# Hash attention and a squared-ReLU layer by two-level Winograd products: an earlier request for the next x, later inner weight factors, and another order in the last output product

## The chip, the cores and the metric

The kernel runs on one core of one Trainium2 chip. The metric is device time in microseconds (us) for one execution, as the median of several runs. The core has TensorE (PE, with its weight loads shown as PEld), VectorE (DVE), ScalarE (ACT), GpSimd (POOL) and SyncE (SP). SP, ACT and POOL issue DMA transfers, each on a queue of its own (in the profile q1, q10 and q0).

## The reference

Attention whose scores are kept only where the hash buckets of query and key agree, then a layer `x @ w_in`, squared ReLU, `@ w_out`:

```python
mask = q_bucket[:, :, :, None] == k_bucket[:, :, None, :]
scores = np.where(mask, scale * np.matmul(q, k.transpose(0, 1, 3, 2)), -1000000000.0)
attn = np.exp(scores - np.max(scores, axis=-1, keepdims=True))
attn = attn / (np.sum(attn, axis=-1, keepdims=True) + 1e-09)
x = (attn @ v).transpose(0, 2, 1, 3).reshape(B * S, H * D)   # 3072 x 512
h = x @ w_in                                                 # 512 x 2048
out = (np.maximum(h, 0.0) ** 2) @ w_out                      # 2048 x 512
```

All tensors are float32. There are 4 batches, 8 heads, 768 positions and 64 features a head; six hash bits come from the signs of `q @ proj` and `k @ proj`.

## The kernel before

The kernel is written out by hand in program order: on every engine the instructions run in the order in which the Python code emits them, and waits on semaphores are put in where a tile is reused or read. Nothing reorders them later.

**Stages.** The first 330 us are attention, two heads at a time. Its result goes to DRAM as `x_all`. Meanwhile the weights are brought into factors for Winograd's form of a block product (seven products and some sums in place of eight products). Then the second layer runs over three chunks of 1024 rows of x (`NCHUNK` is 3, index `i`). A chunk has two parts: the hidden part (`hidden` in the first chunk, `hidden_pair` in the others) makes the squared-ReLU blocks `b11`, `b12`, `b21`, `b22`, `b_t`, and `project(i)` makes the output from them.

**Output products.** `project` runs seven outer products, `k` from 0 to 6 (product 0 to product 6 below). Each is again a Winograd product, made by `product` (L703): seven adds, each of them four matmul calls that use one *leaf* (a 128x512 tile, 256 KB, a factor of `w_out`). An fp32 call shows as two matmuls in the profile, so an add is eight matmuls. The adds take leaves in the order 0, 1, 4, 3, 5, 6, 2 and use three PSUM accumulators; between them ACT copies accumulators out (`one`, `two`, `five`, `three`), and DVE adds them up through `c11`, `c12`, `c22` and `c21`, which stand for the four blocks of the product's result. Leaf n of the chunk (n counts from 0 over all products) is loaded five adds ahead by `load_leaf`, on SP for the first five of a first chunk and on ACT's queue after that; there are seven leaf buffers.

**The hook.** After the second add `product` calls `hook` (L1133). Its first subtraction, `minus(y21, y21, t2)` at L516, makes the right-hand side "t4", which the product's seventh add reads. Then `inner_sums(k + 1)` makes the sums for the next product (three subtractions).

**x and the inner factors.** There is one buffer for x, `load_x(i)` (L551) fills it with 2 MB through POOL's queue, and `sum_x` after products 3 and 4 makes sums of it for the next chunk. From the second chunk on, half of the hidden part is a Winograd product of two levels. Its inner weight factors are made once, in the first chunk's `project`, by `factor_units(n)` (L836) for n from 0 to 3: two loads of 256 KB through POOL into buffers named `h`, four DVE sums (L510 to L513), and four stores to DRAM (L849), again through POOL. `load_inner` reads them back from product 6 on. The `h` buffers are five, taken in turn, and the output blocks use the same ones.

**The end.** In the last product of a chunk (`fourth`) c11 and c12 complete one half of a block of the output and c22 and c21 the other. `close` sends a half when it has both: by a DVE transpose (L1025) and eight small transfers, or, for the second half in the last chunk, by `put_last` (L1037), which transposes on PE, copies on ACT (column 1) and DVE (column 0) and issues two transfers each on SP and ACT.

**Queues.** POOL's queue carries, in this order around the first `project`: stores of the output factors (L1194), the loads of `raw_qk` (L752), then `factor_units` and `load_x`. SP carries `w_unit` (the weights of a hidden step, 640 KB each here), the first leaves and most of the output.

Of the kernel before, what the change touches and what calls it, by code (L numbers as in the profile page):

```python
# [34 lines left out]
def kernel(  # L35
# [31 lines left out]
    NCHUNK = B * S // NCH  # L67
# [14 lines left out]
    HF, HD, NR, NQ = DFF // 2, DM // 2, NFF // 2, NFF // 4  # L82
# [462 lines left out]
    for pr in range(NIN // 2, NP):  # L545
        n = 16 if pr == NP - 1 else 1 + (pr % 3 == 0)
# [4 lines left out]
    def load_x(i):  # L551

        x = p_c.tile([P, NFT, NCH], FP32, name="x")
        nc.gpsimd.dma_start(out=x, in_=x_all[:, :, i * NCH:(i + 1) * NCH])
        xs[i] = x, [p_c.tile([P, 2, NCH // 2], FP32, name=f"t_x{n}") for n in range(3)]
# [36 lines left out]
    with tc.manual_schedule():  # L592
# [21 lines left out]
        for pr in range(NP):  # L614
            a, b = 2 * pr, 2 * pr + 1
            more = pr + 1 < NP
# [83 lines left out]
            p_g.tile([P, NR, HN], FP32, name=f"b{n}") for n in ("11", "12", "21", "22", "_t")  # L700
        )

        def product(n, w, at, bt, c11, c12, c21, c22, hook=None, c22_first=False):  # L703

            acc = [ps_m.tile([P, 512], FP32, name=f"acc{i}")[:, 0:w] for i in range(3)]

            def add(to, a, b, first, last):  # L710
                for i in range(n):
                    nc.tensor.matmul(  # L712
                        out=acc[to], lhsT=a(i), rhs=b(i), start=first and i == 0,
                        stop=last and i == n - 1, skip_group_check=True,
                    )

            def keep(of, name):
                t = p_r.tile([P, 512], FP32, name=name)[:, 0:w]
                nc.scalar.copy(out=t, in_=acc[of])  # L719
                return t  # L720

            add(0, at(0), bt["11"], True, False)
            one = keep(0, "one")
            add(1, at(1), bt["21"], True, True)
            if hook:
                hook()
            c11(acc[1], one)
            add(0, at(4), bt["t2"], False, False)
            two = keep(0, "two")
            add(2, at(3), bt["t1"], True, False)  # L730
            five = keep(2, "five")
            add(0, at(5), bt["t3"], False, False)
            three = keep(0, "three")
            if c22_first:
                c22(three, five)
            add(2, at(6), bt["22"], False, True)
            c12(acc[2], two)
            if not c22_first:
                c22(three, five)
            add(0, at(2), bt["t4"], False, True)  # L740
            c21(acc[0])

# [60 lines left out]
        def new_h():  # L803
            return p_r.tile([P, HN], FP32, name="h", bufs=NH)
# [31 lines left out]
        def factor_units(n):  # L836

            src = [new_h().rearrange("p (a f c) -> p a f c", a=2, c=P) for _ in range(2)]
            for j in range(2):
                nc.gpsimd.dma_start(out=src[j], in_=w_in_7[j * NQ + n, :, 5:7])  # L840
            sums = [new_h().rearrange("p (a f c) -> p a f c", a=2, c=P) for _ in range(2)]
            sums_a(
                src[0][:, :, 0], src[0][:, :, 1], src[1][:, :, 0], src[1][:, :, 1],
                *(sums[j // 2][:, :, j % 2] for j in range(4)),
            )
            for lo, hi, t in (
                (0, 2, src[0]), (2, 3, src[1][:, :, 1:2]), (3, 5, sums[0]), (5, 7, sums[1])
            ):
                nc.gpsimd.dma_start(out=w_in_49[n, :, :, lo:hi], in_=t)  # L849
# [207 lines left out]
        def project(i):  # L1057

            V, W, U, X = (p_y.tile([P, 4, QN], FP32, name=f"sum{n}") for n in range(4))
            outs = {}  # L1060

            def out_block(ih, jh, n):

                row, col = n // 2, n % 2
                if (ih, jh, row) not in outs:
                    outs[ih, jh, row] = [p_y.tile([P, HN], FP32, name="o", bufs=NOUT), 0]
                o = outs[ih, jh, row]
                return o[0][:, col * QN:(col + 1) * QN]

            def close(ih, jh, n):  # L1070
                o = outs[ih, jh, n // 2]
                o[1] += 1
                if (i, ih, jh, n // 2) == (NCHUNK - 1, 1, 0, 1):

                    if o[1] == 2:
                        for col in (1, 0):
                            put_last(n - n % 2 + col, o[0][:, col * QN:(col + 1) * QN])
                elif o[1] == 2:
                    put_out(i, ih, jh, n // 2, o[0])

            def first_(n, one, two):
                if two is None:
                    nc.scalar.copy(out=block(V, n), in_=one)
                else:
                    add_to(block(V, n), one, two)

            def seventh(n, one, two):
                add_to(block(W, n), block(V, n), whole(one, two))

            def fifth(n, one, two):  # L1090
                if two is None:
                    nc.scalar.copy(out=block(U, n), in_=one)
                else:
                    add_to(block(U, n), one, two)

            def third(n, one, two):
                add_to(block(X, n), block(U, n), whole(one, two))
                add_to(block(X, n), block(X, n), block(V, n))

            def second(n, one, two):  # L1100
                add_to(out_block(0, 0, n), block(V, n), whole(one, two))
                close(0, 0, n)

            def sixth(n, one, two):
                t = whole(one, two)
                add_to(out_block(0, 1, n), block(X, n), t)
                close(0, 1, n)
                add_to(block(W, n), block(W, n), t)
                add_to(out_block(1, 1, n), block(W, n), block(U, n))
                close(1, 1, n)  # L1110

            def fourth(n, one, two):
                add_to(out_block(1, 0, n), block(W, n), whole(one, two))
                close(1, 0, n)

            more = i + 1 < NCHUNK
            uses = first_, seventh, fifth, third, second, sixth, fourth
            for k in range(7):
                b = OUTER[k][1]
                t1, t2 = tens.pop(k)  # L1120
                if i == 0 and k < NQ:
                    factor_units(k)
                if k == 6 and more:
                    load_inner(i + 1, 0)
                at = lambda m, k=k: lambda n: leaves[k, m][:, n]
                bt = {
                    "11": lambda n: b[:, n, 0:QN], "21": lambda n: b[:, NQ + n, 0:QN],
                    "22": lambda n: b[:, NQ + n, QN:HN], "t1": lambda n: t1[:, n],
                    "t2": lambda n: t2[:, n], "t3": lambda n: b[:, n, QN:HN],
                    "t4": lambda n: b[:, NQ + n, 0:QN],  # L1130
                }

                def hook():  # L1133
                    y21 = b[:, NQ:NR, 0:QN]
                    minus(y21, y21, t2)
                    if k + 1 < 7 and k not in (1, 3):
                        inner_sums(k + 1)
                    if k == 6 and more:
                        sums_inner(i + 1)

                counted = []

                def a_with_load(m, k=k):
                    load_leaf(7 * k + len(counted) + NLEAF - 2)
                    counted.append(m)
                    return at(m)

                use = uses[k]
                product(
                    NQ, QN, a_with_load, bt, lambda *p: use(0, *p), lambda *p: use(1, *p),  # L1150
                    lambda p: use(2, p, None), lambda *p: use(3, *p), hook, k == 6,
                )
                if k == 0 and i + 1 < NCHUNK:
                    load_x(i + 1)
                if k in (3, 4) and i + 1 < NCHUNK:
                    sum_x(i + 1, 2 * k - 5)
                    sum_x(i + 1, 2 * k - 4)
                if k == 5 and i + 1 == NCHUNK:
                    guard()
                if k == 0:  # L1160

                    for h in range(2):
                        at_h = slice(h * NQ, (h + 1) * NQ)
                        minus(b11[:, at_h], b22[:, at_h], b_t[:, at_h])
                    inner_sums(2)
                if k == 2:

                    for h in range(2):
                        at_h = slice(h * NQ, (h + 1) * NQ)
                        minus(b_t[:, at_h], b21[:, at_h], b11[:, at_h])  # L1170
                    inner_sums(4)
# [315 lines left out]
```

## Time and profile before

| what | us |
|---|---|
| median of 4 runs | 879.29 (878.71 to 880.27) |
| the profiled execution, whole | 879.31 |
| its span, first to last instruction | 877.5 |
| attention, weights | 0 to about 330 |
| hidden part of the first chunk | about 330 to 427.3 |
| output products of the first, second, third chunk start at | 427.3, 606.0, 783.6 |
| last matmul of the output products starts at | 868.4 |

Times in the views below count from the span's start. A row of a timeline has start, duration, engine, line, operation, what it writes and reads, how many instructions are merged in the row, and in brackets how long the engine was idle before it and what ended that. In a chain of waits each row is a start, a duration and the work that the end of the program hung on. Matmul ends are modelled, so the last tenth of a microsecond of a matmul row is not to be read closely.

The issues and landings around the first `project`, from the trace:

| transfer | issued | landed after |
|---|---|---|
| w_unit (SP, 640 KB) | 427.5 | 6.6 |
| leaf 5 | 427.90 | 6.8 |
| leaf 6 | 429.40 | 6.0 |
| leaf 7 | 429.78 | 6.3 |
| leaf 8 | 432.85 | 3.9 |
| stores of unit 0 (POOL, 2 of 256 KB) | 432.87 | 4.5 and 4.8 |
| x for the second chunk (POOL, 2 MB) | 434.00 | 12.2 |
| loads of unit 1 (POOL, 2 of 256 KB) | 434.76 | 12.4 and 12.8 |
| leaf 10 | 436.30 | 7.6 |
| leaf 11 | 436.72 | 9.3 |
| leaf 12 | 439.68 | 8.2 |
| x for the third chunk (POOL) | 614.97 | 12.8 |

### The profile page before, as it was taken

The numbers are of one execution on the slowest core, as the hardware profiler recorded it, in microseconds if no ns is written. First come the engines' busy times: TensorE is split into PE (matmuls) and PEld (weight loads), VectorE is DVE, ScalarE is ACT, GpSimd is POOL, SyncE is SP. The second block draws the span as 40 slices with busy tenths as digits, with TensorE's granted clock in tenths as the row PEclk, the third lists the DMA queues.
The fourth block names the chain that finished last, engine by engine and source line by source line (L and its number), as shares of the span: only waits on it lengthen the run. The fifth ranks groups of instructions, "written<-read, shape, count | busy, mean of one in ns | idle before, by whom it ended". The sixth has DMA issues, their size and how long they took to land.

```text
span 877.5 us, 12127 instructions
## 1 busy us (share of the span) xinstructions
PE 864.7 (99%) x4340; PEld 519.2 (59%) x4340; DVE 760.6 (87%) x1099; ACT 391.7 (45%) x673; POOL 106.9 (12%) x172
## 2 busy tenths in 40 slices
PE   8999999999999999999999999999999999999996
PEld 4444444444444444444688865556888755568885
DVE  5999999999999998888779968888889788888875
ACT  6888888888888852222211123332111233321110
POOL 2000000000000001554231011111000211110002
PEclk9999999999999999999999999999999999999998
DMA  9777977998878526999897764536846744355565
GB/s 174 150 146 133 222 168 150 190 253 226 178 175 227 163 97 220 294 267 284 293 349 240 182 161 167 173 118 222 285 149 188 167 164 155 126 167 151 161 172 108
DMA packets 224131, 167.09 MB, mean 190 GB/s; under 512 B 164448, under 2 KB 181344, under 8 KB 224064
## 3 DMA queue, kind: packets, MB, share of 16 engines
q1 hardware_dynamic: 189152, 87.19, 41.0%
q0 software_dynamic: 12528, 41.30, 15.2%
q10 hardware_dynamic: 22384, 37.76, 13.8%
q8 instruction: 36, 0.59, 0.3%
q14 instruction: 31, 0.25, 0.1%
HBM read 124.52 MB, written 41.68 MB: 189 GB/s over the span
## 4 chain that ended last, share of the span: by engine, by line
PE 95%; DVE 2%; ACT 1%; DMA 1%; issue 0%; POOL 0%; ACTq 0%; POOLq 0%; DVEq 0%
PE acc L712 40%; PE st L396 17%; PE acc L934 16%; PE xo L438 14%; PE acc L887 6%; PE hash L346 2%; PE tot L455 1%; DVE total L428 1%; DMA k_nat<-in_k_dram 1%; ACT bits L356 1%; ACT e L413 0%; PE xo L477 0%; PE tp L309 0%; DVE x_t L493 0%; DVE recs L487 0%
## 5 line engine op out<-in xcount | busy, mean ns | idle before, releaser
L413 ACT ACTIVATE e<-st 128x1024 f32<-128x1024 f32 x192 | 145.0, 810 | 44.9 <-PE st L396 41.0
L396 PE MATMUL st<-feat,feat 64*128 64x512 f32 (+1 forms) x768 | 150.4, 483 | 0.0
L438 PE MATMUL xo<-e,v_nat 128*64 128x512 f32 (+1 forms) x768 | 134.8, 492 | 0.0
L712 PE MATMUL acc<-b,leaf 128*128 128x256 f32 x600 | 133.3, 379 | 1.0 <-issue 1.0
L712 PEld LDWEIGHTS acc<-b,leaf 128*128 128x128 f32 x600 | 113.8, 190 | 17.5 <-issue 2.2
L428 DVE TENSOR_TENSOR total<-total,e 128x1536 f32<-128x1536 f32 x64 | 112.4, 1756 | 8.2 <-ACT e L413 3.6
L438 PEld LDWEIGHTS xo<-e,v_nat 128*64 128x64 f32 x768 | 51.3, 136 | 82.2 <-issue 74.3
L934 PE MATMUL acc<-t_x,w_unit 128*128 128x512 f32 x192 | 90.2, 592 | 0.0
L396 PEld LDWEIGHTS st<-feat,feat 64*128 64x128 f32 x768 | 66.0, 188 | 32.8 <-issue 23.2
L712 PE MATMUL acc<-t,leaf 128*128 128x256 f32 x336 | 76.2, 380 | 0.0
L356 ACT ACTIVATE bits<-hash,lifts 32x384 bf16<-32x384 f32 x120 | 68.7, 573 | 2.3 <-PE hash L346 0.4
L712 PEld LDWEIGHTS acc<-t,leaf 128*128 128x128 f32 x336 | 63.7, 190 | 9.1 <-DVE t L516 0.5
L799 DVE SCALAR_TENSOR_TENSOR b<-h 128x512 f32<-128x512 f32 x96 | 65.7, 692 | 3.0
L396 PE MATMUL st<-bits,bits 64*128 64x256 bf16 (+1 forms) x384 | 63.1, 325 | 1.7 <-ACT e L413 1.2
L934 PE MATMUL acc<-x,w_unit 128*128 128x512 f32 x128 | 60.1, 592 | 0.0
L712 PE MATMUL acc<-x,w_unit 128*128 128x512 f32 x128 | 56.6, 594 | 0.0
L712 PE MATMUL acc<-b_t,leaf 128*128 128x256 f32 x240 | 53.8, 379 | 0.0
L934 PEld LDWEIGHTS acc<-t_x,w_unit 128*128 128x128 f32 x192 | 36.5, 190 | 28.9 <-issue 26.8
L719 ACT COPY two<-acc 128x256 f32<-128x256 f32 (+1 forms) x29 | 12.5, 432 | 87.7 <-PE acc L712 72.2
L719 ACT COPY one<-acc 128x256 f32<-128x256 f32 (+1 forms) x29 | 12.5, 431 | 85.4 <-PE acc L712 56.7
L712 PEld LDWEIGHTS acc<-b_t,leaf 128*128 128x128 f32 x240 | 45.5, 190 | 6.2
L396 PEld LDWEIGHTS <-bits 64*128 64x128 bf16 x384 | 23.6, 93 | 42.5 <-issue 38.4
(159 smaller groups left out, 1166.9 us busy)
## 6 DMA issues: line engine op xcount, KB each, us to landing
leaf<-w_out ACTq DMA_DIRECT2D x142, 256.0 KB, 3.1
w_unit<-w_in SPq DMA_DIRECT2D x16, 640.0 KB, 4.0
raw<-in_moe_w_in_dram SPq DMA_DIRECT2D x16, 512.0 KB, 5.4
raw<-in_moe_w_out_dram SPq DMA_DIRECT2D x16, 512.0 KB, 4.5
w_unit<-w_in SPq DMA_DIRECT2D x8, 896.0 KB, 8.3
w_out<-sums POOLq DMA_DIRECT2D x16, 448.0 KB, 6.8
sum<-w_in SPq DMA_DIRECT2D x16, 448.0 KB, 5.1
v_nat<-in_v_dram SPq DMA_DIRECT2D x16, 384.0 KB, 4.3
```

What stands on the lines that cost most here:

```text
L346: nc.tensor.matmul(out=banks[g * NR_B:(g + 1) * NR_B, h, 0:HS], lhsT=projs[rows], rhs=feat[pr, w][rows, c * HS:(c + 1) * HS], start=True, ...
L356: nc.scalar.activation(out=t[h * D:h * D + NR_B, c * HS:(c + 1) * HS], in_=hashed[pr, w][at, h, 0:HS], func=ACTF.Sign, scale=HUGE, bias=li ...
L396: nc.tensor.matmul(out=st[:, h, 0:hi - lo], lhsT=src[pr, 1][rows, key], rhs=src[pr, 0][rows, lo:hi], start=first, stop=not first,)
L413: nc.scalar.activation(out=e[:, :, lo:hi], in_=sts[i][:, :, 0:hi - lo], func=ACTF.Exp, scale=scale)
L428: nc.vector.tensor_tensor(out=totals[pr], in0=totals[pr], in1=weights[pr, kt][:, :, 0:S], op=ALU.add)
L438: nc.tensor.matmul(out=xo[h * D:(h + 1) * D, lo:hi], lhsT=nat[pr, "v_nat"][:, h, kt * D:(kt + 1) * D], rhs=weights[pr, kt][:, h, lo:hi], s ...
L455: nc.tensor.matmul(out=tot[g * 32:(g + 1) * 32, 0:HS], lhsT=ones, rhs=totals[pr][:, h, c * HS:(c + 1) * HS], start=True, stop=True,)
L712: nc.tensor.matmul(out=acc[to], lhsT=a(i), rhs=b(i), start=first and i == 0, stop=last and i == n - 1, skip_group_check=True,)
L719: nc.scalar.copy(out=t, in_=acc[of])
L799: nc.vector.scalar_tensor_tensor(out=out, in0=h, scalar=0.0, in1=h, op0=ALU.max, op1=ALU.mult)
L887: nc.tensor.matmul(out=out, lhsT=w[:, a], rhs=b, start=start, stop=stop, skip_group_check=True)
L934: nc.tensor.matmul(out=acc[to], lhsT=w[:, PLACE[a], f], rhs=bt[b](f), start=first and f == 0, stop=last and f == NFT // 2 - 1, skip_group_ ...
```

## The change

Three edits. The keyword `c22_first` of `product` goes, so that in product 6 of each chunk `c22` is called after `c12`, as in the other products. `load_x(i + 1)` is called at the beginning of product 0, ahead of everything else of the product, where it was called after product 0. And `factor_units(0)` to `factor_units(3)` are called at the beginning of products 1 to 4, where they were called at the beginning of products 0 to 3.

```diff
-        def product(n, w, at, bt, c11, c12, c21, c22, hook=None, c22_first=False):
+        def product(n, w, at, bt, c11, c12, c21, c22, hook=None):
...
             three = keep(0, "three")
-            if c22_first:
-                c22(three, five)
             add(2, at(6), bt["22"], False, True)
             c12(acc[2], two)
-            if not c22_first:
-                c22(three, five)
+            c22(three, five)
             add(0, at(2), bt["t4"], False, True)
             c21(acc[0])
...
-                if i == 0 and k < NQ:
-                    factor_units(k)
+                if k == 0 and more:
+                    load_x(i + 1)
+                if i == 0 and 0 < k <= NQ:
+                    factor_units(k - 1)
                 if k == 6 and more:
                     load_inner(i + 1, 0)
...
-                    lambda p: use(2, p, None), lambda *p: use(3, *p), hook, k == 6,
+                    lambda p: use(2, p, None), lambda *p: use(3, *p), hook,
                 )
-                if k == 0 and i + 1 < NCHUNK:
-                    load_x(i + 1)
```

In the instruction streams this moves one transfer on POOL (x of the second chunk, from behind the six transfers of unit 0 to ahead of them), four sums on DVE in the first chunk (each unit's four stand one product later, so that four leave the front of product 0 and four are added in front of product 4's hook), and three pairs of rows on DVE, one for each chunk (c22's two adds, behind c12's two adds and its transpose). PE, ACT and SP keep their streams.

## The prediction

> **What bounds the kernel now.** I read the page first, then the waits of PE, then the chain of waits around the output products of the first chunk, then the timelines of DVE and POOL there, then the landings of the leaves, last the tail.
>
> ```profile
> span 877.5 us, 12127 instructions
> ...
> PE 864.7 (99%) x4340; PEld 519.2 (59%) x4340; DVE 760.6 (87%) x1099; ACT 391.7 (45%) x673; POOL 106.9 (12%) x172
> ```
>
> PE works 864.7 of 877.5 us. Matmuls are not touched, so a gain can only come from the 12.8 us in which PE stands, most of it before its first matmul and after its last. Inside, the chain has one break:
>
> ```profile
> 429.87 20.13 PE acc L712 x93
> 450.01 0.95 issue
> 450.96 62.40 PE acc L712 x288
> ```
>
> One add of an output product is 8 matmuls, 62.40/288*8 = 1.73 us; a product is seven adds, 12.1 us. The first matmul of product 0 is at 427.33 (PE's timeline), so product 1 begins at 439.4 and its seventh add is due at 427.33+13*1.73 = 449.8: just where the break is. That add reads the right-hand side "t4", which the hook's first subtraction (L516 b<-b,t) writes. DVE shows why it is late:
>
> ```profile
> 445.44 1.22 DVE L516 TENSOR_TENSOR b_t<-b_t 128x1024 f32<-128x1024 f32 x1
> 448.17 0.43 DVE L510 TENSOR_TENSOR h<-h 128x256 f32<-128x256 f32 x1 [1.51 <-DMA h<-w_in]
> ...
> 449.64 1.22 DVE L516 TENSOR_TENSOR b<-b,t 128x1024 f32<-128x1024 f32 x1
> ```
>
> The subtraction ends at 450.86, and PE starts 0.1 us later. In front of it stand the four sums of factor_units(1) (L510 to L513), and they waited 1.51 us for their load. POOL's timeline tells why that was late: it was issued just behind the 2 MB of the next x.
>
> ```profile
> 434.00 0.95 POOL L554 DMA_DIRECT2D x<-x_all  x1
> 434.76 1.28 POOL L840 DMA_DIRECT2D h<-w_in  x2
> 447.42 0.68 POOL L849 DMA_DIRECT2D w_in<-h  x1 [11.38 <-DMA h<-w_in]
> ```
>
> **Part 1, the stall: -0.95 us.** After the change POOL asks for x before any factor load, and the four sums ahead of product 1's hook are those of unit 0. x can go out when PE has read the old x for the last time, at 427.5 (426.48+1.02, the last matmul of hidden(0,7)); POOL's other wait, an older transfer on its queue, is long over. The two loads of unit 0 follow at 428.5 to 429.6. With the 12.4 and 12.8 us which the same pair took behind x before, they land by 442.4. DVE comes to the sums at 446.66 (445.44+1.22): it gets there no earlier than before, although four sums (1.47 us, from 448.17 to 449.64) leave its queue ahead of product 0, because c12 of product 0 started at 437.96, when PE had finished the sixth add (427.33+6*1.73 = 437.7). So: sums 446.66 to 448.1, hook to 449.35, wanted at 449.8. The stall goes, with 0.45 us to spare. The same chain (c12, c22, two b_t or b subtractions of 4.4, three of inner_sums 3.5, sums 1.47, hook 1.22: 11.4 us against 12.1) stands from product 2 to 3, where the hook ended at 474.69 against 475.1 wanted; it keeps that thin cover. Product 2's sums still wait for their load (3.15 us before); its hook ended at 459.4, wanted at 463.1, and that 3.7 us hides it. Product 4 gets the last four sums: its hook ended at 482.77, wanted at 487.4; 4.6 less 1.47 leaves 3 us. If one of these covers fails, what it is short by is PE's. The inner weights are next read by load_inner before product 6 (about 501), and unit 0 is stored by 454: late by nothing.
>
> For the second chunk nothing moves: ahead of x on POOL stand the loads of raw_qk in both kernels, and x is asked for at 614.97 either way. Bounds of part 1: 0 (hook still late) and -0.95; I take -0.95.
>
> **Part 2, the tail: +0.65 us.** No instruction is added, c22 goes behind c12 in the last product of each chunk. In the first two chunks DVE has the same sum of work before c21, and PE goes on with other work; nothing. At the very end:
>
> ```profile
> 865.82 0.42 DVE L1011 TENSOR_TENSOR tmp<-three,five 128x256 f32<-128x256 f32 x1 [1.22 <-ACT three L719]
> 866.28 0.43 DVE L1011 TENSOR_TENSOR o<-sum,tmp 128x256 f32<-128x256 f32 x1
> 867.09 0.42 DVE L1011 TENSOR_TENSOR tmp<-acc,two 128x256 f32<-128x256 f32 x1 [0.38 <-PE acc L712]
> ...
> 868.00 0.71 DVE L1025 STREAM_TRANSPOSE h<-o 128x512 f32<-128x512 f32 x1
> 868.81 0.42 DVE L1011 TENSOR_TENSOR o<-sum,acc 128x256 f32<-128x256 f32 x1
> ```
>
> The first two rows (c22) ran while DVE waited for PE. Afterwards c12 keeps 867.09 and its transpose 868.00; c22 starts at 868.64 and 869.05 (a row after a transpose starts 0.64 after it, a dependent one 0.41), c21's sum at 869.39 instead of 868.81: +0.58. The transposes of column 1 on PE, at 868.61 before, wait for 869.47, its ACT copy moves from 869.03 to 869.95, and SP's last two issues from 869.69 to 870.36: +0.67. Then follow the landings, SP's flag read, its 3.8 us wait at the branch (waits of SP) and the closing, which hang on these issues. Bounds: 0 (a landing elsewhere hides it) and +0.9 (both rows in full); I take 0.65.
>
> **Part 3, x beside the leaves: +0.4 us.** This is what earlier x collides with. Each add needs one leaf of 256 KB; leaf n is used at 427.33+1.73n. Beside x, in 438 to 446 us, POOL's queue and that of the leaves shared the engines so:
>
> ```profile
> q0 software_dynamic: 602, 2.34, 73.0%
> q10 hardware_dynamic: 475, 0.87, 29.3%
> ...
> leaf<-w_out ACTq DMA_DIRECT2D x5, 256.0 KB, 7.7
> ```
>
> 0.87 MB in 8 us is 109 GB/s where PE eats 256 KB in 1.73 us, 152 GB/s. The reserve was just enough: leaves 10 and 11 (issued 436.30 and 436.72) landed at 443.9 and 446.0, used at 444.6 and 446.4; leaf 12 landed 0.2 us ahead of its use.
>
> ```profile
> DMA to landing us min/median/max: 7.6/8.4/9.3
> ```
>
> (The answer for the leaf issues of 436 to 437 us.) Now leaves 5 to 8 meet x. Without it they took 6.8, 6.0, 6.3 and 3.9 us and had 1.2, 2.3, 3.4 and 4.4 us to spare, with a w_unit of 640 KB (issued 427.53) in SP's queue. Upper end: add what x added to the leaves of the second chunk (3.1 us before it, then 5.0, 7.6, 6.9, 7.3: +1.9, +4.5, +3.8, +4.2). Leaf 6 then lands at 429.4+10.5 = 439.9, used at 437.7: 2.2 us late; PE stands once for the worst, so 2.2. Lower end: the picture of product 1 moved ahead by four adds (6.9 us), where no leaf was late: 0; a gain is excluded, PE has no other stop there. Nearest is the latter, same queues and leaves, but with differences: 640 KB of w_unit in place of 512 KB of unit 0's stores (0.3 us at the 400 GB/s of that stretch, against a reserve of 0.2), and x 0.5 us later against the adds (6.4 us ahead, not 6.9). That makes 0.1 to 0.6; I take 0.4.
>
> [...]
>
> **Sum.** The profiled execution took 879.31 us, 1.8 more than its span, and stands at the median of the runs (879.29). 879.31-0.95+0.65+0.4 = 879.4.
>
> **Rivals.** *Collision, slower*: x delays leaves 6 and 7 so far that PE stands in product 0 or 1 for 2.2 us: 879.31-0.95+0.65+2.2 = 881.2. For: 6.8 us for leaf 5 even without x. Against: the same load in product 1 stopped nothing. It decides from a stop of 2.0 us (0.2% is 1.76 us, about what a measurement of this kernel tells from no change: 881.05 upwards). *It does not do what it says*: the hook of product 1 or 3 misses its 0.4 us of cover and the stall stays in whole or part: 879.31+0.65, up to 880.4. For: covers of 0.45 and 0.4; against: loads with 4 us in hand. *Tail hidden*: another landing ends last, leaves in time: 879.31-0.95 = 878.4. Against: the chain at the end runs through these very rows.
>
> **How the numbers follow.** The forecast (879.4; 878.7 to 880.4 by the bounds 0 to 1 of part 3) 0.55; collision 0.18; stall stays 0.11; tail hidden 0.10. All but the collision lie within 0.2%: 0.76. Faster by 1.76 us would need nearly twice the one break, something like SP's 3.8 us wait becoming shorter: 0.04. Slower 0.18 plus 0.02 unnamed. The range goes from 878.2 (tail hidden, with the 0.6 that the fastest run lay under the median left in part) to 881.2 (collision).
>
> **What would show it.** Right: no break at product 1's seventh add, x issued near 427.6, DVE without a wait before product 1's sums, one short PE stop of 0 to 1 us between 436 and 441, c21's sum 0.6 us later after PE's sixth add of the last product, SP's last issues too. Wrong: PE stops of over 2 us waiting on leaves 5 to 8; unit 0's loads landing after 446; a break at product 3's seventh add; or a span that falls by more than 0.95.

## The result, and the profile after

| | median us | runs from to | executions |
|---|---|---|---|
| before | 879.35 | 878.34 to 881.14 | 52 |
| after | 878.30 | 877.81 to 879.18 | 32 |

The ratio is 0.9988 (95% interval 0.9983 to 0.9993): 1.05 us less, 0.6 to 1.5. The forecast said 0.1 more. The profiled execution of the changed kernel took 878.59 us. Its page begins, in the same columns as before:

```profile
span 876.8 us, 12130 instructions
...
PE 865.0 (99%) x4340; PEld 519.6 (59%) x4340; DVE 760.3 (87%) x1099; ACT 391.8 (45%) x673; POOL 107.0 (12%) x172
```

PE works as long as before, so the gain is idle time of PE. The chain of waits from 425 to 460 us shows which. Where the chain of before broke off at 450.01, this one has a single piece (start, duration, work):

```profile
1 pieces in order of time: start us, us, what
424.68 35.38 PE acc L712 x157
```

From the start of the first chunk's products to that of the second's there were 427.33 to 606.04 = 178.71 us; now there are 427.52 to 605.12 = 177.60. That is 1.11 less, and the span fell by 0.7. Of the 0.4 between, one half is the products' start, 0.19 later in this execution, and the other the end: from the end of the last leaf matmul to the end of the program 8.97 us in place of 8.77.

The timeline of DVE in the changed kernel, ahead of product 1's seventh add:

```profile
445.62 1.22 DVE L516 TENSOR_TENSOR b_t<-b_t 128x1024 f32<-128x1024 f32 x1
446.75 0.42 DVE L510 TENSOR_TENSOR h<-h 128x256 f32<-128x256 f32 x1
...
448.22 1.22 DVE L516 TENSOR_TENSOR b<-b,t 128x1024 f32<-128x1024 f32 x1
```

The second row has no bracket: the four sums follow at once on `inner_sums`, and the hook's subtraction is done at 449.44, ahead of the add. The timeline of POOL shows why the operands were there:

```profile
427.98 0.75 POOL L554 DMA_DIRECT2D x<-x_all  x1 [13.55 <-PE acc L712]
428.72 1.07 POOL L837 DMA_DIRECT2D h<-w_in  x2
440.53 0.70 POOL L846 DMA_DIRECT2D w_in<-h  x1 [10.73 <-DMA h<-w_in]
```

x is asked for 6.0 us earlier and landed after 11.1. The two loads behind it landed at 440.25 and 441.19 (the store of the first, last row, follows at once): still 11.5 and 11.9 us for 256 KB each, but now 5.6 us ahead of their sums.

The leaves that meet x on the DMA engines, in the profile's view of the tile `leaf` on ACT's queue, issues of 429.6 to 430.0 (leaves 6 and 7), 433.0 (8) and 434.8 (9):

```profile
DMA to landing us min/median/max: 6.7/7.5/8.4
...
DMA to landing us min/median/max: 7.4/7.4/7.4
...
DMA to landing us min/median/max: 6.8/6.8/6.8
```

They did get slower, yet leaves 5 to 9 landed 3.78, 1.65, 1.25, 0.92 and 1.52 us ahead of their use. PE has no stop between 436 and 446.

One small delay is left that the waits of PE do not list. Counted from start to start, product 3's seventh add begins 0.16 us late, spread over its first two matmuls. DVE reaches the subtraction which that add needs only at 472.90:

```profile
456.36 0.42 DVE L510 TENSOR_TENSOR h<-h 128x256 f32<-128x256 f32 x1 [4.05 <-DMA h<-w_in]
...
472.90 1.22 DVE L516 TENSOR_TENSOR b<-b,t 128x1024 f32<-128x1024 f32 x1
```

Between these two rows DVE has no idle time, so the landing of unit 1's load, ahead of product 2's hook, still sets product 3's hook.

At the end of the kernel DVE's timeline has c22 (L1008 `tmp<-three,five`) behind c12 and its transpose, as the diff says, and SP's last issue comes later after PE's last leaf matmul:

```profile
866.23 0.42 DVE L1008 TENSOR_TENSOR tmp<-acc,two 128x256 f32<-128x256 f32 x1 [2.55 <-PE acc L712]
...
867.15 0.71 DVE L1022 STREAM_TRANSPOSE h<-o 128x512 f32<-128x512 f32 x1
867.79 0.38 DVE L1008 TENSOR_TENSOR tmp<-three,five 128x256 f32<-128x256 f32 x1
...
868.55 0.41 DVE L1008 TENSOR_TENSOR o<-sum,acc 128x256 f32<-128x256 f32 x1
```

From c12's first add to c21's sum there are 868.55-866.23 = 2.32 us, where before there were 868.81-867.09 = 1.72: +0.60.

### The profile page after: what moved, and what is told of

The parts are those of the page before. It is cut to its first block, busy times and chain, and to the rows that moved or that the text cites. A ratio compares the mean times of both kernels' runs of the same rounds, so it can differ in the third digit from the quotient of the medians.

```text
span 876.8 us, 12130 instructions
## 1 busy us (share of the span) xinstructions
PE 865.0 (99%) x4340; PEld 519.6 (59%) x4340; DVE 760.3 (87%) x1099; ACT 391.8 (45%) x673; POOL 107.0 (12%) x172
## 4 chain that ended last, share of the span: by engine, by line
PE 96%; DVE 2%; ACT 1%; issue 0%; DVEq 0%; ACTq 0%
PE acc L712 40%; PE st L396 17%; PE acc L931 16%; PE xo L438 14%; PE acc L884 6%; PE hash L346 2%; PE tot L455 1%; DVE total L428 1%; ACT bits L356 1%; PE xo L326 0%; ACT e L413 0%; PE tp L309 0%; PE xo L477 0%; DVE x_t L493 0%; DVE recs L487 0%
```

## The experiments

Each kernel is compared with the kernel before, run on the same chip. Three questions: is the gain the stop alone; what does the new order at the end cost; and why did x not delay the leaves?

### The parts one by one

The order at the end alone (`tail_alone`, an edit of the kernel before):

```diff
-    lambda p: use(2, p, None), lambda *p: use(3, *p), hook, k == 6,
+    lambda p: use(2, p, None), lambda *p: use(3, *p), hook,
```

> The kernel before with one edit: in the last product of each chunk c22 stands behind c12, as in the changed kernel. Theory (the order at the end costs what the rows on DVE, PE and SP show, measured from PE's last add of the output): SP's last issue comes 0.65 us later after PE's end, time +0.65 us, about 880.0. Rival (the end of the program is set by SP's wait at the branch and the closing, and hides the shift): SP's last issue moves all the same, time +0.0 to +0.2, about 879.4.

Measured: 879.92 (879.64 to 881.24) against 879.56, ratio 1.0005 (0.9996 to 1.0014). +0.4 us by the medians, and the interval does not exclude nothing. SP's last issue ends 2.54 us after the end of the last leaf matmul, against 1.90 in the profile of before.

The other two edits without the end (`after_c22`, the changed kernel with `c22_first` restored; `product` takes the keyword again, not shown):

```diff
-    lambda p: use(2, p, None), lambda *p: use(3, *p), hook,
+    lambda p: use(2, p, None), lambda *p: use(3, *p), hook, k == 6,
```

> The changed kernel with the old order kept in its last product (c22 ahead of c12): the x and factor edits alone. Theory (order at the end costs 0.65): 0.65 us under the changed kernel, about 877.65, that is 1.7 under the kernel before, of which 1.1 is the stop at product 1's seventh add in the profiled run and the rest the same stop being longer in other runs. Rival (the end hides the order): as the changed kernel, 878.3.

Measured: 878.22 (877.76 to 878.9), ratio 0.9982 (0.9973 to 0.9991), that is -1.6 us (-0.8 to -2.4). The gain is near the theory's -1.7; the time itself lies nearer the rival's 878.3, and the changed kernel's runs were not beside these. No stop at product 1, none at the leaves.

The two edits of the first chunk can be split no further. With the factors one product later, POOL gets no instruction between the beginning and the end of product 0, so x stands at the same place of its queue whether it is asked for at the one or at the other. The earlier request by itself then does nothing; what puts x ahead of the factor loads is that these move.

### How steady the stop is

Both kernels profiled once more, unchanged:

> The kernel before, unchanged, for a second profile. Theory (the stop at product 1's seventh add hangs on when unit 1's loads land behind x, and so differs between executions): a stop at the same add, longer or shorter than the 0.95 idle us of the first profile by some tenths to 1 us, with DVE's wait for h<-w_in longer or shorter by as much. Rival (a fixed cost): 0.95 again within 0.1.

> The changed kernel, unchanged, for a second profile. Theory (leaves 5 to 9 keep about 1 us in hand beside x): again no stop of PE in products 0 and 1, the least reserve of a leaf between 0.3 and 1.5 us. Rival (the first profile was lucky): a stop of 0.2 to 1 us between 436 and 443.

Measured: before 880.72 (span 879.0), after 879.1 (span 877.3). In the second profile of before the chain of waits around the same place reads

```profile
424.62 26.07 PE acc L712 x112
450.69 1.82 issue
452.51 7.58 PE acc L712 x34
```

and DVE's timeline

```profile
449.72 0.42 DVE L510 TENSOR_TENSOR h<-h 128x256 f32<-128x256 f32 x1 [2.51 <-DMA h<-w_in]
...
451.19 1.22 DVE L516 TENSOR_TENSOR b<-b,t 128x1024 f32<-128x1024 f32 x1
```

DVE waited for the same load 1.00 us longer than in the first profile, and PE stood 0.87 longer. In the profile of `tail_alone` DVE waited 1.75 and PE 1.26. So the break is 0.95, 1.26 and 1.82 us in three profiles, and the forecast took the shortest. It is also counted from a modelled end. From start to start the same two matmuls are 1.12, 1.42 and 1.98 us further apart than their neighbours, and a few starts beside the stop are late as well. From the first chunk's products to the second's there are 178.71, 178.95 and 179.70 us with the stop, and 177.45 in `after_c22`, where no start is late. So the stop costs 1.26, 1.50 and 2.25 us, 1.67 on the mean. In three profiles of the changed kernel (the third is `after_b`, below) there are 177.60, 177.87 and 177.61, so that it gains 1.43 on the mean. That may be high, because one of the three executions with the stop took 880.72 us, well above the median. The standard deviation of the runs above is 0.62 us before and 0.32 after, which would fit a stop that hangs on a landing; but on the chip of `after_c22_b`, below, it is 0.44 with the stop and 0.44 without.

The second profile of after has one wait of PE between 430 and 500 us (waits of PE: who waited for what, us in total, times, longest):

```profile
PE acc L712 <- issue: 0.2, 1, 0.2
```

It ends at 474.76, with product 3's seventh add: the place where the forecast saw a cover of 0.4 us only. From start to start that add is 0.42 us late here, 0.16 in each of `after` and `after_b`, and on time in `after_c22`, `after_c22_b` and `tail_longer`. The landing of unit 1's load tells them apart: from the first matmul of the products to product 2's sums, which wait for it, there are 28.85 to 29.11 us in the three with the delay and 28.48 to 28.55 in the others. Only the spread of the landing is between them, as this stretch of the program is the same in all six.

### Is it DVE's queue, or the landing?

If the stop arises because the hook's subtraction stands behind the four sums, it must go when the subtraction passes in front, however late the load lands. `sums_behind_hook` leaves x and the units of before where they are and puts a unit's sums and stores behind the subtraction:

```diff
-            sums = [new_h()... for _ in range(2)]
-            sums_a(...)
-            for lo, hi, t in (...):
-                nc.gpsimd.dma_start(out=w_in_49[n, :, :, lo:hi], in_=t)
+            def rest():
+                sums = [new_h()... for _ in range(2)]
+                sums_a(...)
+                for lo, hi, t in (...):
+                    nc.gpsimd.dma_start(out=w_in_49[n, :, :, lo:hi], in_=t)
+            return rest
...
-                    factor_units(k)
+                rest = factor_units(k) if i == 0 and k < NQ else None
...
                     minus(y21, y21, t2)
+                    if rest:
+                        rest()
```

> The kernel before, its x and its loads where they were; only the four DVE sums of a unit (and its stores) stand behind the hook's first subtraction and no longer ahead of it. Theory (PE stopped because that subtraction stood behind sums that waited for a load): no stop at product 1's seventh add although the loads land as late as before, 1.1 to 1.7 us less, 877.7 to 878.3. Rival (the late landing of what is behind x reaches PE in another way, or the leaves did it): the stop stays, 879.3.

Measured: 878.63 (878.25 to 880.52) against 879.48, ratio 0.9992 (0.9983 to 1.0001): above the expected 877.7 to 878.3, and the interval does not exclude nothing. Its timeline of DVE:

```profile
447.19 1.22 DVE L516 TENSOR_TENSOR b<-b,t 128x1024 f32<-128x1024 f32 x1
449.37 0.43 DVE L510 TENSOR_TENSOR h<-h 128x256 f32<-128x256 f32 x1 [0.96 <-DMA h<-w_in]
```

The load lands as late as before (DVE waits for it until 449.37, later than the 448.17 of the first profile of before), but the subtraction is over by then, and PE has no wait between 430 and 500 us. So the place of the subtraction in DVE's queue makes the stop, and the landing sets its length. From the first chunk's products to the second's there are 177.45 us, as in `after_c22`, so in its profile the whole stop is gone. (The stores of unit 0 come later here and push x back by 1.1 us against the products, from 434.00 to 435.75 on the clock of each profile.) The 0.85 us by the medians is less than the stop; why is open.

### The order of x and the units

`x_alone` asks for x at the beginning of product 0 and leaves the units where they were, so that unit 0's two loads stand behind x:

```diff
+                if k == 0 and more:
+                    load_x(i + 1)
                 if i == 0 and k < NQ:
                     factor_units(k)
...
-                if k == 0 and i + 1 < NCHUNK:
-                    load_x(i + 1)
```

> The kernel before with x asked for at the beginning of product 0, the factor units where they were: unit 0's loads then stand behind x and its sums ahead of product 0's hook. Theory (what stands behind x on the queue lands some 12 us later, and DVE's queue holds the hook behind it): loads land at about 441, product 0's hook ends at about 444 where 437.7 is wanted, a stop of 6 us, and one of about 3 at product 1, in all 8 us more, about 887.5. Rival (x early is what helps, the units' place does not matter): 878.3 to 879.

Measured: 889.04 (887.78 to 890.95), ratio 1.0109 (1.0092 to 1.0127), +9.6 us by the ratio. DVE and then PE in its profile:

```profile
442.58 0.43 DVE L510 TENSOR_TENSOR h<-h 128x256 f32<-128x256 f32 x1 [10.28 <-DMA h<-w_in]
```

```profile
445.37 7.43 PE L712 MATMUL acc<-b,leaf 128*128 128x256 f32 x24 [6.79 <-issue]
```

The same stop, at the seventh add of product 0, and 6.79 us long. A second one, at product 1's seventh add, is 0.73 long where about 3 were expected.

`x_behind_unit1` puts x behind the loads and stores of unit 1 instead, with one product more of delay for x:

```diff
                     factor_units(k)
+                if k == (1 if i == 0 else 0) and more:
+                    load_x(i + 1)
```

> The kernel before with x asked for later: behind all of unit 1 at the beginning of product 1. Theory: the stop at product 1 is gone (-1.1), but now unit 2's loads stand behind x, land at about 462, product 2's hook ends at about 465 where 462 is wanted: a new stop of 2 to 3.5 us at product 2's seventh add, net +1 to +2.4, about 880.3 to 881.7. Rival (the next load has time enough wherever x is): -1.1, 878.2.

Measured: 885.92 (885.19 to 886.3), ratio 1.0069 (1.0054 to 1.0084), +6.1 by the ratio, where +1 to +2.4 were expected: a miss. The stop moved one product on, to product 2's seventh add, and is 4.37 us long; DVE waited 11.48 us for unit 2's load, now the one behind x. A second stop of 1.05 us stands at product 3's seventh add. In every order with one x the two loads behind it on POOL's queue land 11.4 to 13.8 us after their issue; whether PE stops hangs on the distance from these loads to their sums.

### Do the leaves have room?

`x_twice` is the changed kernel with the second chunk's x loaded twice, one load after the other, so that the leaves meet 4 MB in place of 2:

```diff
-        nc.gpsimd.dma_start(out=x, in_=x_all[:, :, i * NCH:(i + 1) * NCH])
+        for _ in range(2 if i == 1 else 1):
+            nc.gpsimd.dma_start(out=x, in_=x_all[:, :, i * NCH:(i + 1) * NCH])
```

> The changed kernel with the second chunk's x loaded twice, one load behind the other (the second 2 MB are not needed). Theory (the leaves run at about 130 KB a us beside x against 152 that PE eats, so a reserve of 1 us lasts another 6 to 8 us): unit 0's loads land near 449 instead of 441, product 1's hook ends at about 452 to 453 where 450 is wanted, and the leaves come up to 0.5 late: a stop of 2 to 3.5 us, about 880.3 to 881.8. Rival (collision as forecast, the leaves lose 4 us of reserve for each x): leaves 10 to 13 come 2 us or more late, stops before product 1's seventh add, 882 or more.

Measured: 884.4 (882.65 to 888.69), ratio 1.0058 (1.0036 to 1.0081). By time that is the rival's "882 or more" and not the theory's 880.3 to 881.8, but the stop is the one of the theory, only longer, and not on a leaf: the leaves keep at least 1.2 us, and those issued ahead of the stop would have kept it without the stop too. (In `after` ACT's queue carried 1.45 MB from 430 to 441 us, 132 KB a us, near the 130 of the expectation.) PE stands 4.17 us ahead of product 1's seventh add, because the factor loads stand behind both loads of x and land at 450.60 and 451.70 (440.25 and 441.19 in `after`), and DVE waited 4.67 us for them. A second stop of 0.8 us stands in the second chunk's hidden part, at 521, on a load of the inner factors. In this run the price of another x is paid through POOL's queue, not through the leaves.

### What the end costs

The changed kernel with and without the old order at the end, once more on another chip, with a third that makes the end longer:

```diff
             def fourth(n, one, two):
+                for _ in range(4 if (i, n) == (NCHUNK - 1, 3) else 0):
+                    whole(one, two)
                 add_to(out_block(1, 0, n), block(W, n), whole(one, two))
```

(`tail_longer`; the four added adds repeat c22's first, ahead of c21.)

> The changed kernel with c22 ahead of c12 in its last product, a second time, beside the changed kernel on one chip. Theory (the later order moves SP's last issues by 0.65 us, of which SP's shorter wait at the branch takes back about 0.4): 0.2 to 0.4 us under the changed kernel. Rival (0.65 in full): 0.6 to 0.7 under it. Other rival (nothing): within 0.1.

> The changed kernel, unchanged, as the yardstick for the run above: 878.3, between 878.0 and 878.7, with less scatter than the kernel before (no stop that hangs on a landing).

> The changed kernel with four more DVE adds (the first add of c22's last block, done five times) ahead of c21's sum in the last chunk: the suspected cost of the tail made longer by 4 times 0.36 to 0.46, 1.4 to 1.8 us. Theory (once SP's branch wait is at its shortest, some 3.3 us, the tail passes to the end in full): SP's last issue and the end both 1.4 to 1.8 later, 879.7 to 880.1. Rival (the wait at the branch goes on shrinking with the later branch): the issue is later by as much, the end by a third to a half, 878.8 to 879.2.

Measured: `after_c22_b` 878.35 (ratio 0.9990, 0.9981 to 0.9999), `after_b` 878.56 (0.9993, 0.9984 to 1.0002), `tail_longer` 879.26 (1.0000, 0.999 to 1.0009). From the end of the last leaf matmul, by the traces:

| end of | old order: before, before_again, after_c22, after_c22_b | new order: after, after_again, tail_alone, after_b | tail_longer |
|---|---|---|---|
| SP's last issue | 1.90, 1.84, 1.84, 1.92 | 2.53, 2.54, 2.54, 2.54 | 3.94 |
| the program | 8.77, 8.64, 8.58, 8.47 | 8.97, 8.95, 8.70, 9.13 | 9.49 |

SP's last issue moves by 0.66 on the mean, the end by 0.32; the other four profiles fit (end 8.39 to 8.68 in the old order, 8.89 in `x_twice`). In `tail_longer` the issue moves by 1.40 more and the end by 0.55. Where the rest stays is in SP's own waits from 860 to 880 us. In the kernel before, at the branch behind the last issues:

```profile
SPq L1286 <- SPq L1286: 3.8, 1, 3.8
```

in `after_b` and in `tail_longer`:

```profile
SPq L1283 <- SPq L1283: 3.5, 1, 3.5
```

```profile
SPq L1285 <- SPq L1285: 2.6, 1, 2.6
```

Over the table's profiles the wait is 3.5 to 3.8 in the old order, 3.2 to 3.5 in the new one and 2.6 in `tail_longer`. It gets shorter as the branch comes later: in `tail_longer`, with the issue 1.40 us later, by 0.6 to 0.9 us against the new order. `tail_longer` costs 0.70 us over `after_b` where the wait as a fixed length would have made 1.4 or more: the rival was right in kind, and its 878.8 to 879.2 just too low.

## Why the forecast was wrong

**Part 1 (-0.95): the stall right, its size too small, and one cover read wrongly.** x went out at 427.98 (forecast 427.6 or near), the loads landed at 441.2 (by 442.4), DVE came to the sums at 446.75 (446.66) without a wait, the hook ended at 449.44 (449.35), and DVE's 1.39 us wait for product 0's sixth add, which was to absorb the four sums taken from the front, is in the trace at 438.15. The failed step is the price: 0.95 was read off the break in one profile, where the products lost 1.26 from start to start, and that execution had the shortest stop of three. The stop cost 1.67 on the mean, and 0.24 of it came back at product 3. There the step that failed is "that 3.7 us hides it": the cover of product 2's hook hides the wait for unit 1's load from product 2 only. DVE works without a gap from the end of that wait to product 3's hook, 17.75 us later, and in three of six profiles that add of product 3 came 0.16 to 0.42 us late. The distance between the chunks' products fell by 1.43 on the mean, and the two edits without the end took 1.6 and 0.9 us off the time by their ratios, 1.2 on the mean.

**Part 2 (+0.65): the shift right, its worth at the end too large.** SP's last issue came 0.66 later (0.67 worked out), c21's sum 0.60 (0.58). The step that failed is "which hang on these issues": it took the 3.8 us at the branch as a length that moves along. It shrinks (3.5 to 3.8 us before, 3.2 to 3.5 after), and about half of the shift arrives: +0.32 in the traces, +0.36 between the medians of `tail_alone` and before, +0.21 between those of `after_b` and `after_c22_b`. No interval of these runs separates it from nothing; only the traces agree on it.

**Part 3 (+0.4): wrong; it is nothing.** The failed step is the picture that was moved ahead. Leaves 6 to 8 were to have the reserve of product 1's leaves, 0.2 us, and to lose 0.3 of it to the larger w_unit and up to 0.5 to the later x. In the trace they took 6.7, 8.4 and 7.4 us where leaves 10 to 12 had taken 7.6, 9.3 and 8.2, and kept at least 0.92. Nor was w_unit longer in the way than unit 0's stores: it landed 3.7 us after x was issued, where in the kernel before the stores had landed 3.4 and 4.2 us after x was. Which of the differences made the leaves quicker was not tried. The base of the upper end, "Without it they took 6.8, 6.0, 6.3 and 3.9 us", was one execution as well. There w_unit took 6.6 us and leaf 5 landed 1.25 us ahead of its use. In the second profile of before w_unit took 4.4 and leaves 5 to 8 had 3.34, 4.30, 5.41 and 5.28 us to spare; in after w_unit took 3.9 and leaf 5 4.3. A slow w_unit and x did come together once, in the second profile of after: w_unit took 6.1, leaves 6 to 9 took 7.0 to 8.8, and leaves 5 to 9 had 2.12, 1.27, 0.87, 0.44 and 0.30 us to spare. That x slows the leaves is right, then, and the room is thin, but in none of five profiles of kernels with these two edits (`after`, `after_again`, `after_b`, `after_c22`, `after_c22_b`) was a leaf late.

**The sum** from what the runs show: -1.43 in the products of the first chunk (leaves included), +0.32 at the end, -1.1; measured -1.05 (-0.6 to -1.5). Three profiles a side make the -1.43 uncertain by some tenths, so that the sum comes this close is in part luck. The forecast's +0.1 had its two costs too high by 0.3 and 0.4 and its gain too low by some 0.5.

**The rivals.** The collision is refuted: no stop at a leaf, not even with x doubled. "The stall stays" is refuted for product 1; its second half, product 3, came true in part, with 0.16, 0.42 and 0.16 us in three of those five profiles. "Tail hidden" (878.4) is the nearest in time, but only half by its mechanism: another wait swallows about half of the shift, and the end still moves by some 0.3. The span fell by 0.7, less than the 0.95 that was to speak against the sum; so the sign by span did not uncover that two of its terms were off.

The version with both edits of the first chunk and the old order at the end (`after_c22`) is the fastest measured: 0.9982 and 0.9990 of before. Its 0.1 and 0.2 us over the changed kernel are inside the intervals.

## What to carry to other kernels

When an in-order engine makes side work out of a transfer, look at what is queued behind that work: here the stop went when the urgent instruction was put in front, and when the work was put one stage later, with the transfer as slow as before. Follow such a wait past the first instruction that it delays: without idle time behind it, it reaches later ones too. A stop that hangs on a landing had no single size here (1.26, 1.50 and 2.25 us), so take it from several profiles before it enters a sum. Don't carry the reserve of one place over to another either, and don't take one execution's late landing as the rule. A shift of the last issues was not the same shift of the end (0.66 and 0.32 us here); look for a wait behind them that can shrink.

## What the hardware showed unexpectedly

**The longer stops cost more than themselves.** In `x_alone` the next matmuls behind the stop start mostly 0.43 us apart in place of 0.22, and over ten starts that adds 2.1 us to it. The table of stretches of `x_alone` shows why (stretch, its length, busy us and count of PE, PEld, DVE, ACT, POOL, then the granted clock of PE, the DMA share and GB/s):

```profile
438.00:445.00 7.00, 0.58 (x3) 0.17 (x1) 2.39 (x5) 0.00 (x0) 2.43 (x4) 0.83 0.87 321
445.00:450.00 5.00, 4.63 (x12) 3.80 (x13) 4.97 (x8) 0.37 (x1) 2.11 (x4) 0.55 0.66 210
450.00:460.00 10.00, 9.71 (x45) 8.20 (x44) 9.93 (x10) 1.49 (x4) 1.72 (x4) 1.00 0.66 188
```

After the stop of 6.79 us the granted clock is 0.55 over the next 5 us and 12 matmuls take 4.63 us; from 450 to 460 us it is 1.00, with 45 in 9.71. The stop of 4.17 us in `x_twice` did the same, that of 1.82 us in the second profile of before did not:

```profile
455.00:459.00 4.00, 4.00 (x12) 3.21 (x11) 2.15 (x6) 0.00 (x0) 1.32 (x3) 0.58 0.75 223
```

```profile
455.00:459.00 4.00, 4.00 (x20) 3.54 (x19) 1.36 (x5) 0.37 (x1) 1.61 (x3) 1.00 0.80 263
```

In the same 4 us PE made 12 matmuls at a clock of 0.58 in the first and 20 at 1.00 in the second. Behind the stop of 4.37 us in `x_behind_unit1` it made 13 at 0.58 from 467 to 471, behind the 0.95 us of before 20 at 1.00 from 455 to 459. No run here has a stop of between 1.82 and 4.17 us in the output products.

**The wait at SP's branch shrinks**, from 3.8 to 2.6 us, when the branch comes later. What it waits for is not shown. It is not the last landing alone: in `tail_alone` SP goes on 0.17 us before ACT's last transfer has landed. In the profile of before 4 packets (0.03 MB) of an instruction queue (q14) move from 871.4 to 875.2 us, while SP waits, and in `after` 3 (0.02 MB) from 871.2 to 874.6; no run here tells whether the wait hangs on them.
